# Casts of head pairs 2 to 5 on VectorE, and the first loads of batch 1 and the first-half weights re-ordered, in a hash-attention kernel with a maxout FFN

## The chip, the cores and the metric

The kernel runs on one core of one Trainium2 chip. The metric is the device time of one execution in microseconds (us); lower is better. Engine names: PE is TensorE (PEld its weight loads), DVE is VectorE, ACT is ScalarE, POOL or Pool is GpSimd, SP is SyncE, used here only to issue DMAs. Quoted times are medians of several executions. A ratio is the mean time of one kernel's fast runs over the mean of the other's fast runs in the same rounds, so it is not quite the ratio of the quoted medians. "Fast" leaves out executions more than 1.5% above the fastest of the same kernel. A profile is one execution; its span is 1.7 to 1.8 us shorter than the time measured for it.

## The reference

Inputs are q, k, v of 4 batches x 8 heads x 768 positions x 64, a random projection of 64 x 6, and FFN weights. Positions attend only where the six sign bits of q and k projected agree.

```python
def _attn_ref(q, k, v, proj):
    q_bits = (np.einsum('bhsd,dk->bhsk', q, proj) > 0)
    k_bits = (np.einsum('bhsd,dk->bhsk', k, proj) > 0)
    # ... bucket = sum of bits * powers of two
    mask = q_bucket[:, :, :, None] == k_bucket[:, :, None, :]
    scores = np.where(mask, scale * np.matmul(q, k.transpose(0, 1, 3, 2)), -1e9)
    attn = np.exp(scores - scores.max(-1, keepdims=True))
    attn = attn / (attn.sum(-1, keepdims=True) + 1e-09)
    return np.matmul(attn, v)

def _moe_ref(x, w1, w2, w3, w_out):        # x: 3072 x 512
    h = np.maximum(np.maximum(x @ w1, x @ w2), x @ w3)
    return h @ w_out
```

## The kernel before

The work runs in 16 head pairs, numbered 0 to 15 (four per batch). While pair n goes through its score matmuls and exponentials, the kernel finishes the softmax of pair n-1, hashes pair n+1, and transposes and casts the operands of pair n+2. FFN matmuls of a finished batch fill PE from pair 4 on. A pair has 12 units (one 768-wide exponential each on ACT), and `add(u, f, ...)` places a piece of work behind unit u. The kernel schedules by hand, and in the timelines below the instructions of an engine come in this program order.

Three chains matter here. The first is the operand of a pair: DMA to `nat`, transpose to `tf` (fp32), then a cast to bf16 into the operand tile.

```python
    def load(nm, b, j):                    # batches 1 to 3: four DMAs on the Pool queue
        t = natp.tile([P, 4, R * D // 4], FP32, tag=nm + "nat", name=nm + "nat")
        for hd in (0, 1):
            # ...
                nc.gpsimd.dma_start(t[32 * g : 32 * g + 32, ...], s[...])

    def convert(nm, b, j, cs=slice(0, S), copy=nc.gpsimd.tensor_copy):
        for hd in (0, 1):
            copy(oset(b, j)[nm, hd][head_rows(hd), cs], tf[nm, b, j][head_rows(hd), cs])
```

The second is the hash: matmul into two PSUM banks, threshold on DVE into `bt`, then eight small DMAs (12 x 384 bf16 each) on the SP queue into spare rows of the operand tiles. The second half's writes are needed from the second unit of the pair on.

```python
    def hash_pair(b, j):
        # ... 16 matmuls into ps[0], ps[1]
        for half in (0, 1):
            nc.vector.tensor_scalar(out=bt[:, half_cols(half)], in0=ps[half][:, 0:HS], ...)
            for hd in (0, 1):
                for z, nm in enumerate(("q", "k")):
                    nc.sync.dma_start(oset(b, j)[nm, hd][...], bt[...])
```

The third is the softmax denominator: ones-matmuls on PE, eviction `ds` on ACT, a reciprocal `rc` on DVE, eight tiny copies `r` on Pool, a broadcast `rb` on DVE, and the scaled product `xT` on DVE.

```python
    def den_rc(ph):
        nc.vector.transpose(dT..., rcb.pop(ph)[:])
        # ...
        nc.vector.reciprocal(rc[:], rc[:])
        for half in (0, 1):
            # ... four copies per half
                    nc.gpsimd.tensor_copy(r2[o : o + 32, :], rc[s : s + 32, :])
```

`hold` is a tiny Pool copy which reads what a DMA wrote, and so keeps everything behind it on the Pool queue back until that DMA has landed. `hold` at the end of pair 0 is called "the gate" below: it waits for the last hash write of pair 1 before the first loads of batch 1 are issued.

```python
        if ph == 0:
            # ...
            add(11, hold, (oset(0, 1)["k", 1][0:1, S - 1 : S], slice(0, 1)))
            add(11, load, "k", 1, 0)
            add(11, load, "q", 1, 0)
        elif ph == 1:
            add(5, load_v, 0, 1)
            add(5, load, "k", 1, 1)
            add(5, load, "q", 1, 1)
            for m in range(3):
                add(7, load_weight, m, 0)
        elif ph == 2:
            add(6, load_v, 0, 2)
            add(6, load_v, 0, 3)
        elif ph == 3:
            # ... loads of pair 6, then
            for m in range(3):
                add(7, load_weight, m, 1)
```

The softmax here doesn't subtract the row's maximum and nothing guards it: scores larger than these inputs give would overflow.

Of the kernel before, what the change touches and what calls it, by code (L numbers as in the profile page):

```python
# [17 lines left out]
def kernel(  # L18
# [12 lines left out]
    nc = tc.nc  # L31
    B, H, S, D = q.shape
# [4 lines left out]
    HS = S // 2  # L37
# [4 lines left out]
    NPAIR = H // 2  # L42
# [23 lines left out]
    def half_cols(half):  # L66
        return slice(half * HS, half * HS + HS)

    def head_rows(hd):
        return slice(D * hd, D * hd + D)  # L70
# [99 lines left out]
    def oset(b, j):  # L170
        return opd[(b * NPAIR + j) % NSET]
# [30 lines left out]
    def split_psum(wide):  # L202
        psx.close()
        n = 1 if wide else 2
        extra = psx.enter_context(tc.tile_pool(name=f"psx{n}", bufs=n, space=bass.MemoryType.PSUM))
        sc_ring.clear()
        sc_ring.extend((psp, psp, extra) if wide else (psp, psp))
        bank_ring.clear()
        bank_ring.extend((psw, psw) if wide else (psw, psw, extra, extra))
# [34 lines left out]
        src = nat[nm, b, j][:].rearrange("p pg (c x) -> p c pg x", x=D)[:, :, :, 0:32]  # L244
        nc.vector.transpose(dst.rearrange("p (c pg i) -> p c pg i", pg=4, i=32), src)  # L245

    def convert(nm, b, j, cs=slice(0, S), copy=nc.gpsimd.tensor_copy):
        for hd in (0, 1):
            copy(oset(b, j)[nm, hd][head_rows(hd), cs], tf[nm, b, j][head_rows(hd), cs])  # L249

# [36 lines left out]
    def qk_unit(ph, b, j, half, c):  # L287
        sc = psum2()
        for hd in (0, 1):
            rows = KROWS[hd]  # L290
            kT = oset(b, j)["k", hd]
            qT = oset(b, j)["q", hd]
            nc.tensor.matmul(sc[:, hd, 0:HS], kT[rows, c * P : c * P + P],  # L293
                             qT[rows, half * HS : half * HS + HS], start=True, stop=True)
        nc.scalar.activation(atile(ph, half, c)[:, :, 0:HS], sc[:, :, 0:HS], ActFn.Exp, scale=SCALE)  # L295
# [120 lines left out]
    h0, h1 = half_cols(0), half_cols(1)  # L416
    vcopy, acopy = nc.vector.tensor_copy, nc.scalar.copy
    pe_transpose("k", 0, 0, 0, vcopy)
    pe_transpose("q", 0, 0, 0, acopy)
    hash_first("k", 0)  # L420
    convert("k", 0, 0, h0, acopy)
    hash_first("q", 0)
    convert("q", 0, 0, h0, acopy)
    pe_transpose("k", 0, 0, 1, vcopy)
    pe_transpose("q", 0, 0, 1, acopy)
# [3 lines left out]
    for ph, (b, j) in enumerate(pairs):  # L429
        todo = {u: [] for u in range(NU)}  # L430

        def add(u, f, *a):
            todo[u].append(lambda: f(*a))

        def prep(nb, nj):
            if nb == 0:
                for u, nm, half in ((4, "k", 0), (5, "k", 1), (6, "q", 0), (8, "q", 1)) if ph else ((7, "k", 0), (8, "k", 1), (9, "q", 0), (10, "q", 1)):
                    add(u, pe_transpose, nm, nb, nj, half, nc.vector.tensor_copy)
                    if half == 1:
                        add(u, convert, nm, nb, nj)  # L440
            else:
                for u, nm in zip((1, 5) if ph < NPAIR else (8, 10), ("k", "q")):
                    add(u, transpose, nm, nb, nj)
                    add(u, convert, nm, nb, nj)

        if ph > 0:
            pb, pj = pairs[ph - 1]
            sparse = ph <= NPAIR
            if sparse:
                add(2, den_mm, ph - 1, 0, NT3)  # L450
                add(3, den_mm, ph - 1, NT3, NCH)
                add(4, den_rc, ph - 1)
                add(5, den_rb, ph - 1, 0)
                add(6, den_rb, ph - 1, 1)
                if ph == NPAIR:
                    add(7, split_psum, False)
                add(7, av, ph - 1, pb, pj, 0)
                add(9, av, ph - 1, pb, pj, 1)
            else:
                add(1, den_mm, ph - 1, 0, NCH)  # L460
                add(2, den_rc, ph - 1)
                add(4, den_rb, ph - 1, 0)
                add(5, den_rb, ph - 1, 1)
                add(6, av, ph - 1, pb, pj, 0)
                add(6, av, ph - 1, pb, pj, 1)
        if ph == 0:
            add(0, hold, nat["q", 0, 1][:, 0:1])
            add(0, load_v, 0, 0)
            add(3, load0, "k", 3, nc.gpsimd)
            add(3, load0, "q", 3, nc.gpsimd)  # L470
            add(11, hold, (oset(0, 1)["k", 1][0:1, S - 1 : S], slice(0, 1)))
            add(11, load, "k", 1, 0)
            add(11, load, "q", 1, 0)
        elif ph == 1:
            add(5, load_v, 0, 1)
            add(5, load, "k", 1, 1)
            add(5, load, "q", 1, 1)
            for m in range(3):
                add(7, load_weight, m, 0)
        elif ph == 2:  # L480
            add(6, load_v, 0, 2)
            add(6, load_v, 0, 3)
        elif ph == 3:
            add(6, load, "k", *pairs[6])
            add(6, load, "q", *pairs[6])
            for m in range(3):
                add(7, load_weight, m, 1)
        elif ph + 3 < len(pairs):
            add(6, load, "k", *pairs[ph + 3])
            add(6, load, "q", *pairs[ph + 3])  # L490
            if ph == 4:
                add(8, load_wo)
        if 4 <= ph + 1 < len(pairs):
            add(9, load_v, *pairs[ph + 1])
        if 0 < ph and ph + 1 < len(pairs):
            add(0 if ph <= NPAIR else 1, hash_pair, *pairs[ph + 1])
        if ph + 2 < len(pairs):
            prep(*pairs[ph + 2])
        u = 0
        order = [(c, half) for c in range(NCH) for half in (0, 1)]  # L500
        if ph == 0:
            order = [(c, half) for half in (0, 1) for c in range(NCH)]
            add(0, hash_first, "k", 1)
            add(0, convert, "k", 0, 0, h1)
            for i, (nm, half) in enumerate((("k", 0), ("k", 1), ("q", 0), ("q", 1))):
                add(2 + i // 2, pe_transpose, nm, 0, 1, half, vcopy if half == 0 else acopy)
            add(1, hash_first, "q", 1)
            add(1, convert, "q", 0, 0, h1)
            add(4, hash_pair, 0, 1)
            add(4, convert, "k", 0, 1)  # L510
            add(4, convert, "q", 0, 1)
        if ph == 1:
            split_psum(True)
        for c, half in order:
            qk_unit(ph, b, j, half, c)
            for f in todo[u]:
                f()
            left = len(pairs) * NU - (ph * NU + u)
            quota = (ffn_left[0] - TAILW) / left
            spent = 0.0  # L520
            while ffn and spent + ffn[0][0] / 2 <= quota:
                cost, f = ffn.popleft()
                f()
                spent += cost
            ffn_left[0] -= spent
            u += 1
# [41 lines left out]
```

## Time and profile before

| | before |
|---|---|
| time at the prediction | 301.31 us median (300.43 to 301.68) |
| span of the profile | 298.9 us |
| PE busy | 281.0 us (94%) |
| DVE, ACT, POOL busy | 159.5, 191.7, 152.9 us |
| PE busy from 100 to 220 us | 119.75 of 120 us |

First the page of the kernel before: busy us with share of the span and instructions, then rows of 40 equal slices of the span, one digit each (busy tenths for PE and POOL, granted TensorE clock in tenths for PEclk).

```profile
PE 281.0 (94%) x2220; PEld 146.4 (49%) x2220; DVE 159.5 (53%) x346; ACT 191.7 (64%) x290; POOL 152.9 (51%) x353
...
PE   7987897985999899999999999999999999999994
...
POOL 7698895696776575748373938384252020200000
PEclk9999797996999999999999999999999999999999
```

Behind the tenth slice (75 us) PE is full. Only the front has room, and there Pool is the engine with the high digits.

Next the table of windows of the kernel before: start:end, length, then busy us of PE, PEld, DVE, ACT and POOL with their instruction counts, the granted clock (1.00 is full), the DMA engines' busy share and GB/s.

```profile
24.00:28.00 4.00, 3.67 (x40) 1.80 (x38) 1.27 (x4) 3.96 (x7) 3.64 (x8) 1.00 0.59 153
28.00:32.00 4.00, 1.99 (x16) 1.45 (x17) 2.10 (x5) 1.57 (x3) 3.66 (x13) 0.92 1.02 221
32.00:36.00 4.00, 4.00 (x25) 1.90 (x22) 1.46 (x4) 1.63 (x2) 3.22 (x6) 0.65 1.09 217
48.00:52.00 4.00, 4.00 (x28) 1.00 (x32) 2.29 (x4) 0.88 (x2) 1.94 (x3) 0.57 0.57 80
56.00:60.00 4.00, 4.00 (x43) 1.84 (x40) 3.24 (x7) 3.58 (x6) 3.09 (x9) 1.00 0.03 7
68.00:72.00 4.00, 1.43 (x5) 0.71 (x5) 2.71 (x5) 0.75 (x2) 3.53 (x11) 0.62 1.32 207
72.00:76.00 4.00, 4.00 (x20) 1.58 (x18) 0.79 (x3) 1.36 (x2) 0.94 (x3) 0.53 1.21 235
```

Three times PE idles and the clock then falls to about half. Each half-clock stretch costs again, since a PE that is 4.00 of 4.00 busy at 0.53 does about half the work: a score matmul takes 0.53 us there and 0.33 at full clock.

The PE timeline of the kernel before shows what ended these waits, and a shorter one for a hash write (start us, length, engine, line, operation, output <- inputs; in brackets the idle time before it and its releaser):

```profile
23.62 0.32 PE L293 MATMUL sc<-qop_1_171,kop_1_169 128*128 128x384 bf16 x1 [0.71 <-DMA qop_1_171<-bt]
...
30.89 0.35 PE L346 MATMUL wk<-at_181,v 128*64 128x385 f16 x2 [1.84 <-DVE ktf L239]
47.94 1.66 PE L271 MATMUL wk<-qtf,pmq 64*32 64x384 f32 x6 [1.62 <-DVE sv L349]
70.57 0.48 PE L364 MATMUL wk<-xT,w_sb 128*128 128x384 f16 x1 [3.40 <-DVE xT L352]
```

And the Pool timeline of the kernel before shows why DVE was late, with `r` the reciprocal copies:

```profile
24.48 2.22 POOL L97 DMA_DIRECT2D knat<-in_k_dram  x4
26.69 2.19 POOL L97 DMA_DIRECT2D qnat<-in_q_dram  x4
28.87 0.91 POOL L330 COPY r_522<-rc 32x12 f32<-32x12 f32 x4
...
43.48 0.83 POOL L249 CAST kop_1_169<-ktf 64x768 bf16<-64x768 f32 x1
44.37 0.89 POOL L330 COPY r_718<-rc 32x12 f32<-32x12 f32 x4
...
66.62 0.70 POOL L105 DMA_DIRECT2D v<-in_v_dram  x1 [0.56 <-DMA knat<-in_k_dram]
67.36 0.89 POOL L330 COPY r_1046<-rc 32x12 f32<-32x12 f32 x4
```

The reciprocals were ready at 27.7, 42.1 and 64.8 us. The copies started 1.2, 2.3 and 2.5 us later, behind load issues, casts, and a v load whose issue had to wait for an earlier load to land.

### The profile page before, as it was taken

The numbers are of one execution on the slowest core, as the hardware profiler recorded it, in microseconds if no ns is written. First come the engines' busy times: TensorE is split into PE (matmuls) and PEld (weight loads), VectorE is DVE, ScalarE is ACT, GpSimd is POOL, SyncE is SP. The second block draws the span as 40 slices with busy tenths as digits, with TensorE's granted clock in tenths as the row PEclk, the third lists the DMA queues.
The fourth block names the chain that finished last, engine by engine and source line by source line (L and its number), as shares of the span: only waits on it lengthen the run. The fifth ranks groups of instructions, "written<-read, shape, count | busy, mean of one in ns | idle before, by whom it ended". The sixth has DMA issues, their size and how long they took to land.

```text
span 298.9 us, 6145 instructions
## 1 busy us (share of the span) xinstructions
PE 281.0 (94%) x2220; PEld 146.4 (49%) x2220; DVE 159.5 (53%) x346; ACT 191.7 (64%) x290; POOL 152.9 (51%) x353
## 2 busy tenths in 40 slices
PE   7987897985999899999999999999999999999994
PEld 3543442432455445554555555554555455555551
DVE  4843546534575718573675547672757063725250
ACT  3787395982568695868767776768676966131322
POOL 7698895696776575748373938384252020200000
PEclk9999797996999999999999999999999999999999
DMA  7945997089996293719282848276012020020202
GB/s 174 170 114 144 216 176 111 15 200 220 208 182 138 69 242 94 165 30 203 114 197 33 194 142 196 37 163 168 14 29 37 27 81 2 0 105 2 106 0 106
DMA packets 26718, 34.54 MB, mean 116 GB/s; under 512 B 10080, under 2 KB 20736, under 8 KB 26688
## 3 DMA queue, kind: packets, MB, share of 16 engines
q0 software_dynamic: 14704, 24.39, 40.7%
q1 hardware_dynamic: 9648, 8.85, 9.7%
q10 hardware_dynamic: 2336, 0.92, 1.4%
q8 instruction: 17, 0.28, 0.4%
q14 instruction: 13, 0.11, 0.1%
HBM read 33.03 MB, written 6.29 MB: 132 GB/s over the span
## 4 chain that ended last, share of the span: by engine, by line
PE 81%; POOL 7%; DVE 4%; DMA 4%; issue 1%; ACT 1%; SPq 0%; ACTq 0%; DVEq 0%; POOLq 0%
PE wk L364 32%; PE sc L293 18%; PE wk L380 10%; PE wk L346 10%; PE wk L309 5%; PE wk L271 4%; DMA knat<-in_k_dram 2%; DMA pr<-in_proj_dram 1%; POOL knat L97 1%; PE wk L238 1%; PE wk L256 1%; POOL w_sb L188 1%; POOL qnat L97 1%; DVE qtf L245 1%; DMA kop_1_169<-bt 1%
## 5 line engine op out<-in xcount | busy, mean ns | idle before, releaser
L364 PE MATMUL wk<-xT,w_sb 128*128 128x384 f16 x576 | 111.9, 327 | 3.9 <-DVE xT L352 3.4
L364 PEld LDWEIGHTS <-w_sb 128*128 128x128 f16 x576 | 54.4, 98 | 46.2 <-issue 11.3
L274 DVE TENSOR_SCALAR bt<-wk,thrqk,fac 128x384 bf16<-128x384 f32 x30 | 18.9, 673 | 44.0 <-PE wk L271 44.0
L346 PEld LDWEIGHTS <-v 128*64 128x64 f16 x384 | 21.3, 112 | 16.6 <-issue 9.1
L97 POOL DMA_DIRECT2D qnat<-in_q_dram x48 | 26.3, 553 | 4.9 <-DMA w_sb<-in_moe_w_dram 3.1
L97 POOL DMA_DIRECT2D knat<-in_k_dram x48 | 26.5, 559 | 0.0
L293 PE MATMUL sc<-qop_0_168,kop_0_167 76*128 76x384 bf16 x72 | 24.0, 333 | 1.9 <-ACT at_183 L295 0.6
L293 PE MATMUL sc<-qop_0_165,kop_0_163 128*128 128x384 bf16 x72 | 23.9, 332 | 0.3 <-ACT qtf L239 0.3
L394 ACT COPY o<-wk 128x512 f32<-128x512 f32 x23 | 13.5, 586 | 13.8 <-PE wk L380 13.2
L293 PE MATMUL sc<-qop_1_174,kop_1_173 76*128 76x384 bf16 x60 | 20.5, 341 | 0.9 <-POOL kop_2_179 L249 0.5
L293 PE MATMUL sc<-qop_1_171,kop_1_169 128*128 128x384 bf16 x60 | 20.4, 340 | 0.7 <-DMA qop_1_171<-bt 0.7
L293 PE MATMUL sc<-qop_2_180,kop_2_179 76*128 76x384 bf16 x60 | 19.7, 328 | 0.4 <-ACT at_185 L295 0.4
L293 PE MATMUL sc<-qop_2_177,kop_2_175 128*128 128x384 bf16 x60 | 19.6, 327 | 0.0
L320 DVE STREAM_TRANSPOSE dT<-ds 128x384 f32<-128x384 f32 x16 | 9.2, 572 | 14.7 <-ACT ds L315 14.7
L271 PE MATMUL wk<-qtf,pmq 64*32 64x384 f32 x120 | 14.8, 509 | 1.6 <-DVE sv L349 1.6
L309 PEld LDWEIGHTS <-ones_157 128*32 128x32 f16 x384 | 8.8, 96 | 10.2 <-issue 7.2
L271 PE MATMUL wk<-ktf,pmk 64*32 64x384 f32 x120 | 13.4, 518 | 0.0
L295 ACT ACTIVATE at_188<-sc 128x768 f16<-128x768 f32 x8 | 6.7, 836 | 9.8 <-PE sc L293 9.8
L295 ACT ACTIVATE at_200<-sc 128x768 f16<-128x768 f32 x8 | 6.6, 821 | 9.8 <-PE sc L293 9.8
L293 PEld LDWEIGHTS <-kop_1_173 76*128 76x128 bf16 x60 | 6.0, 99 | 12.7 <-issue 8.2
L349 DVE TENSOR_SCALAR sv<-wk 128x1 f32<-128x1 f32 x32 | 4.9, 153 | 13.2 <-PE wk L346 13.2
L105 POOL DMA_DIRECT2D v<-in_v_dram x16 | 11.6, 727 | 0.6 <-DMA knat<-in_k_dram 0.6
(481 smaller groups left out, 672.1 us busy)
## 6 DMA issues: line engine op xcount, KB each, us to landing
knat<-in_k_dram POOLq DMA_DIRECT2D x48, 176.0 KB, 3.7
qnat<-in_q_dram POOLq DMA_DIRECT2D x48, 176.0 KB, 4.9
out_dram<-o SPq DMA_DIRECT2D x7, 768.0 KB
v<-in_v_dram POOLq DMA_DIRECT2D x16, 192.0 KB, 3.6
w_sb<-in_moe_w_dram POOLq DMA_DIRECT2D x6, 384.0 KB, 7.5
wo_sb<-in_moe_w_out_dram POOLq DMA_DIRECT2D x1, 768.0 KB, 8.6
out_dram<-o SPq DMA_DIRECT2D x2, 256.0 KB
knat_94<-in_k_dram SPq DMA_DIRECT2D x2, 192.0 KB
```

The source lines that it names most:

```text
L97: nc.gpsimd.dma_start(t[32 * g : 32 * g + 32, :, 0 : NCH * D - 32], s[:, :, 32 * blk : 32 * blk + NCH * D - 32])
L105: nc.gpsimd.dma_start(t[:].rearrange("p h c d -> p h (c d)"), v[b, 2 * j : 2 * j + 2].rearrange("h (p c) d -> p h (c d)", p=P))
L271: nc.tensor.matmul(ps[half][o : o + 32, 0:HS], pm[nm][head_rows(hd), :], tf[nm, b, j][head_rows(hd), half_cols(half)], start=True, stop=True)
L274: nc.vector.tensor_scalar(out=bt[:, half_cols(half)], in0=ps[half][:, 0:HS], scalar1=thr["qk"][:, 0:1], scalar2=fac[:, 0:1], op0=AluOp.is_ ...
L293: nc.tensor.matmul(sc[:, hd, 0:HS], kT[rows, c * P : c * P + P], qT[rows, half * HS : half * HS + HS], start=True, stop=True)
L295: nc.scalar.activation(atile(ph, half, c)[:, :, 0:HS], sc[:, :, 0:HS], ActFn.Exp, scale=SCALE)
L309: nc.tensor.matmul(ps[32 * g : 32 * g + 32, 0:HS], ones32[:], atile(ph, half, c)[:, hd, 0:HS], start=(c == 0), stop=(c == NCH - 1))
L320: nc.vector.transpose(dT[:].rearrange("p a x -> p (a x)"), rcb.pop(ph)[:])
L346: nc.tensor.matmul(ps[D * hd : D * hd + D, 0 : HS + 1], vv[:, hd, c, :], atile(ph, half, c)[:, hd, :], start=(c == 0), stop=(c == NCH - 1))
L364: nc.tensor.matmul(ps[:, 0:HS], w_sb[m, fb // NT3][:, jc, (fb % NT3) * P : (fb % NT3) * P + P], xT[b][:, jc, half * HS : half * HS + HS], ...
L380: nc.tensor.matmul(ps[:, 0:DM], hts[b, half, fb][:, t * P : t * P + P], w_sb["o"][:, fb, :], start=(fb == 0), stop=(fb == NFB - 1))
L394: nc.scalar.copy(o[:, t, :], ps[:, 0:DM])
```

## The change

The intent is to empty the Pool queue where the reciprocal copies stand in it. Casts of pairs 2 to 5 go to DVE. The q load of batch 1's first pair goes behind the copies. The gate opens on the first half's hash write, so that the k load need not wait for the second. First-half weights move from pair 1 to pair 2, in front of v of pairs 2 and 3; second-half weights move one unit later in pair 3. (The casts of pair 1 and of half of pair 0 stay on Pool; they are named explicitly because the default changed.)

```diff
--- before.py
+++ after.py
@@ -244,7 +244,9 @@
         src = nat[nm, b, j][:].rearrange("p pg (c x) -> p c pg x", x=D)[:, :, :, 0:32]
         nc.vector.transpose(dst.rearrange("p (c pg i) -> p c pg i", pg=4, i=32), src)
 
-    def convert(nm, b, j, cs=slice(0, S), copy=nc.gpsimd.tensor_copy):
+    def convert(nm, b, j, cs=slice(0, S), copy=None):
+        if copy is None:
+            copy = nc.vector.tensor_copy if b * NPAIR + j < 6 else nc.gpsimd.tensor_copy
         for hd in (0, 1):
             copy(oset(b, j)[nm, hd][head_rows(hd), cs], tf[nm, b, j][head_rows(hd), cs])
 
@@ -468,23 +470,23 @@
             add(0, load_v, 0, 0)
             add(3, load0, "k", 3, nc.gpsimd)
             add(3, load0, "q", 3, nc.gpsimd)
-            add(11, hold, (oset(0, 1)["k", 1][0:1, S - 1 : S], slice(0, 1)))
+            add(11, hold, (oset(0, 1)["k", 1][0:1, HS - 1 : HS], slice(0, 1)))
             add(11, load, "k", 1, 0)
-            add(11, load, "q", 1, 0)
         elif ph == 1:
+            add(5, load, "q", 1, 0)
             add(5, load_v, 0, 1)
             add(5, load, "k", 1, 1)
             add(5, load, "q", 1, 1)
+        elif ph == 2:
             for m in range(3):
-                add(7, load_weight, m, 0)
-        elif ph == 2:
+                add(6, load_weight, m, 0)
             add(6, load_v, 0, 2)
             add(6, load_v, 0, 3)
         elif ph == 3:
             add(6, load, "k", *pairs[6])
             add(6, load, "q", *pairs[6])
             for m in range(3):
-                add(7, load_weight, m, 1)
+                add(8, load_weight, m, 1)
         elif ph + 3 < len(pairs):
             add(6, load, "k", *pairs[ph + 3])
             add(6, load, "q", *pairs[ph + 3])
@@ -501,14 +503,14 @@
         if ph == 0:
             order = [(c, half) for half in (0, 1) for c in range(NCH)]
             add(0, hash_first, "k", 1)
-            add(0, convert, "k", 0, 0, h1)
+            add(0, convert, "k", 0, 0, h1, nc.gpsimd.tensor_copy)
             for i, (nm, half) in enumerate((("k", 0), ("k", 1), ("q", 0), ("q", 1))):
                 add(2 + i // 2, pe_transpose, nm, 0, 1, half, vcopy if half == 0 else acopy)
             add(1, hash_first, "q", 1)
-            add(1, convert, "q", 0, 0, h1)
+            add(1, convert, "q", 0, 0, h1, nc.gpsimd.tensor_copy)
             add(4, hash_pair, 0, 1)
-            add(4, convert, "k", 0, 1)
-            add(4, convert, "q", 0, 1)
+            add(4, convert, "k", 0, 1, slice(0, S), nc.gpsimd.tensor_copy)
+            add(4, convert, "q", 0, 1, slice(0, S), nc.gpsimd.tensor_copy)
         if ph == 1:
             split_psum(True)
         for c, half in order:
```

## The prediction

> **What bounds it now.** The page gives PE 281.0 of 298.9 us busy (94%); the chain of waits is 81% PE. From 100 us to 220 us the table of windows shows PE busy 119.75 of 120. So the back is PE-bound; a gain can only come from the front, pairs 1 to 4 (21 to 80 us), where PE idles and loses its clock. The same table shows the granted clock at 0.50 to 0.85 in 30-36, 48-52 and 68-76 us, each time after an idle stretch.
>
> Why PE idles: the Pool queue is in order and nearly full in pairs 1 to 4 (13.2 of 15.3, 8.7 of 9.4, 7.6 of 13.1, 16.3 of 21.5 us). The small reciprocal copies (8 x 0.19 us) wait behind casts (0.83 us) and DMA issues (0.55 to 0.77 us):
> - Pair 1: reciprocal ready 27.7, copies start 28.87 behind eight load issues; PE idles 28.9-30.9, then runs at half clock.
> - Pair 2: ready 42.1, copies 44.37, behind casts and weight issues; the next hash starts 47.94 (1.6 us idle, then half clock).
> - Pair 4: ready 64.8, copies 67.36. Pool was held at 66.3 until a k load eight issues earlier had landed. PE waits 3.4 us for xT (ACT 4.7), and the clock is 0.50 until 75 us.
>
> **What changes.** 16 casts of 64x768 (pairs 2 to 5; 16 x 0.88 = 14 us) leave Pool; DVE gets 16 copies. No such DVE copy is in the trace. The Trainium skill ("VectorE: DVE Perf Modes", Mode 2x_2P) says a single-source SBUF-to-SBUF copy runs two elements a cycle even for fp32: estimate 0.5 us each, 8 us in all; at one a cycle, 0.9. DVE is 42 to 65% busy in these pairs, but the casts sit between the reciprocal work and the evictions. "SBUF — State Buffer" (two separate sides) says such a copy and a Pool instruction exclude each other; no trace here shows it yet; I allow 1 us. Moreover: q of batch 1's first pair is issued after the copies; the gate waits for the first half's hash write (about 3 us sooner); first-half weights go behind pair 2's copies. Total DMA work is unchanged.
>
> **By stage (estimates from these times).**
> - Pair 1: copies 1.1 us earlier, no clock drop, hash at about 35 instead of 36.85.
> - Pair 2: copies when the reciprocal is ready (40.2); end of the next hash 46.5 instead of 50.2.
> - Pair 3: the added DVE casts stand before the second rb and xT: gives back about 1 us.
> - Pair 4: copies at about 62 instead of 67.4; first FFN block 65 instead of 70.6 (5.5 us), plus up to 2.6 us of half clock.
> Behind that everything is shifted, not changed. Gain 5 to 8.5 us, less contention: 6.7 us.
>
> **Predicted:** 294.6 us, 8 in 10 between 290.8 and 299.5. Faster by over 2%: 0.55; within: 0.42; slower: 0.03.
>
> **What would show it.** DVE casts of about 0.5 us; Pool's wait in pairs 1 to 4 for the reciprocal rather than the reverse; PE's 3.4 us wait for xT under 2; clock 1.00 in 30-36 and 48-52 us; PE still near 120 of 120 in the middle.
>
> **What would make it wrong.** DVE casts of 0.9 us or more, from no fast mode or from Pool holding the port, making DVE the new wait for rb and xT. Earlier k loads colliding with the second-half hash writes (needed at pair 1's second unit). Loads for pair 2's v queued behind 1.2 MB of weights (about 6 us) and landing after need (near 51 us). PE's gap before the FFN still long enough to halve the clock.

## The result, and the profile after

| | before | after |
|---|---|---|
| time, rounds of the prediction | 301.22 us (300.43 to 301.68) | 297.17 us (296.63 to 297.81) |
| ratio of fast runs, 95% interval | | 0.987 (0.984 to 0.990) |
| span of the profile | 298.9 us | 295.9 us |
| PE busy | 281.0 us | 279.6 us |
| DVE busy | 159.5 us | 169.5 us |
| POOL busy | 152.9 us | 140.6 us |

The kernel was 1.3% faster in these rounds. Two later sets, on two different chips, gave 0.997 (0.993 to 1.002) and 0.993 (0.988 to 0.997) for the same two kernels, so the gain is somewhere between nothing and 1.3%. All are "within 2%".

The page of the changed kernel, the same rows as above:

```profile
PE 279.6 (95%) x2220; PEld 145.7 (49%) x2220; DVE 169.5 (57%) x362; ACT 191.8 (65%) x290; POOL 140.6 (48%) x337
...
PE   8978798798999999999999999999999999999994
...
POOL 7591855567684847566573937383242020200000
PEclk9997999799999999999999999999999999999999
```

The clock dips at other places now, at the fourth and eighth slice. The table of windows of the changed kernel:

```profile
24.00:28.00 4.00, 3.05 (x21) 0.81 (x24) 0.84 (x2) 1.58 (x3) 0.00 (x0) 0.62 0.42 98
32.00:36.00 4.00, 2.97 (x27) 1.70 (x28) 3.85 (x9) 1.82 (x3) 3.96 (x8) 1.00 0.56 142
48.00:52.00 4.00, 3.68 (x42) 1.24 (x46) 2.91 (x6) 2.38 (x5) 0.72 (x2) 1.00 1.31 204
56.00:60.00 4.00, 4.00 (x26) 1.75 (x24) 3.24 (x7) 1.23 (x2) 3.96 (x9) 0.61 0.58 157
72.00:76.00 4.00, 4.00 (x31) 2.28 (x28) 2.61 (x5) 2.56 (x5) 2.96 (x5) 1.00 1.06 236
```

All three old stretches (32, 48, 72 us) run at 1.00. But 24-28 us and 56-60 us, full speed before, are now at 0.62 and 0.61. The PE timeline of the changed kernel shows two waits that did not exist, or were half as long:

```profile
24.95 0.48 PE L295 MATMUL sc<-qop_1_171,kop_1_169 128*128 128x384 bf16 x1 [1.38 <-DMA qop_1_171<-bt]
...
48.31 1.32 PE L273 MATMUL wk<-qtf,pmq 64*32 64x384 f32 x6 [1.01 <-DVE sv L351]
...
55.78 0.53 PE L348 MATMUL wk<-at_181,v 128*64 128x385 f16 x2 [1.38 <-DMA v<-in_v_dram]
...
69.99 0.32 PE L366 MATMUL wk<-xT,w_sb 128*128 128x384 f16 x1 [0.86 <-DVE xT L354]
```

The chain of waits of the changed kernel names the transfers behind them (start us, length, what):

```profile
21.51 3.40 DMA qop_1_171<-bt
...
47.27 8.46 DMA v<-in_v_dram
```

The first is the hash write of pair 1's second half. Before, the same write was issued at 21.70 and PE stopped waiting for it at 23.62, so it took at most 1.9 us. In 23 to 25 us, while PE waited for this write or had just got it, the windows of the changed kernel show the DMA engines 1.00 and 0.98 busy, where the kernel before shows 0.07 and 0.04. The second is v of pair 2, queued behind the three weight loads. The Pool timeline of the changed kernel:

```profile
21.05 0.32 POOL L180 CAST gate<-kop_1_169 1x1 f32<-1x1 bf16 x1
21.32 2.35 POOL L97 DMA_DIRECT2D knat<-in_k_dram  x4
30.43 0.88 POOL L332 COPY r_517<-rc 32x12 f32<-32x12 f32 x4 [6.76 <-DVE rc L325]
...
43.31 0.86 POOL L332 COPY r_712<-rc 32x12 f32<-32x12 f32 x4 [1.59 <-DVE rc L325]
45.05 2.27 POOL L188 DMA_DIRECT2D w_sb<-in_moe_w_dram  x3
47.27 1.45 POOL L105 DMA_DIRECT2D v<-in_v_dram  x2
...
66.82 0.87 POOL L332 COPY r_1046<-rc 32x12 f32<-32x12 f32 x4 [2.99 <-DVE rc L325]
```

Pool now waits for the reciprocal everywhere, so the change did what it meant to do. But the reciprocals themselves come late: pair 1's copies begin at 30.43 instead of 28.87, and pair 4's at 66.82, only 0.5 us before the old 67.36. The k load now issues at 21.32, exactly while the hash writes of 21.51 are under way.

Where the 3.0 us of span came from can be read off one point, the first score matmul of pair 5: 78.29 us before, 75.28 after. Behind it both profiles take 220.6 us (298.9 - 78.29 and 295.9 - 75.28). The first FFN block that waits for `xT` in pair 4 moved only 0.6 us (70.57 to 69.99); the other 2.4 us are the clock that no longer halves at 70-76 us.

### The profile page after: what moved, and what is told of

Same layout as the page of the kernel before. It is cut to its first block, busy times and chain, and to the rows that moved or that the text cites. A ratio compares the mean times of both kernels' runs of the same rounds, so it can differ in the third digit from the quotient of the medians.

```text
span 295.9 us, 6133 instructions
## 1 busy us (share of the span) xinstructions
PE 279.6 (95%) x2220; PEld 145.7 (49%) x2220; DVE 169.5 (57%) x362; ACT 191.8 (65%) x290; POOL 140.6 (48%) x337
## 4 chain that ended last, share of the span: by engine, by line
PE 80%; DMA 5%; DVE 5%; POOL 4%; ACT 2%; issue 1%; SPq 1%; DVEq 0%; POOLq 0%; ACTq 0%
PE wk L366 32%; PE sc L295 17%; PE wk L382 11%; PE wk L348 10%; PE wk L311 5%; DMA v<-in_v_dram 4%; PE wk L273 3%; PE sc L417 1%; DMA qop_1_171<-bt 1%; POOL qnat L97 1%; SPq L282 1%; POOL w_sb L188 1%; DVE dT L322 1%; PE wk L258 1%; POOL qnat_337 L89 1%
## 5 line engine op out<-in xcount | busy, mean ns | idle before, releaser
L97 POOL DMA_DIRECT2D qnat<-in_q_dram x48 | 26.9, 566 | 2.4 <-DMA v<-in_v_dram 1.5
L295 PE MATMUL sc<-qop_1_171,kop_1_169 128*128 128x384 bf16 x60 | 20.2, 336 | 1.4 <-DMA qop_1_171<-bt 1.4
L273 PE MATMUL wk<-ktf,pmk 64*32 64x384 f32 x120 | 12.8, 495 | 0.0
L295 PEld LDWEIGHTS <-kop_0_167 76*128 76x128 bf16 x72 | 7.1, 98 | 9.5 <-issue 5.7
L245 DVE STREAM_TRANSPOSE ktf<-knat 128x768 f32<-128x768 f32 x12 | 11.6, 970 | 0.0
```

The source lines that it names most:

```text
L97: nc.gpsimd.dma_start(t[32 * g : 32 * g + 32, :, 0 : NCH * D - 32], s[:, :, 32 * blk : 32 * blk + NCH * D - 32])
L273: nc.tensor.matmul(ps[half][o : o + 32, 0:HS], pm[nm][head_rows(hd), :], tf[nm, b, j][head_rows(hd), half_cols(half)], start=True, stop=True)
L295: nc.tensor.matmul(sc[:, hd, 0:HS], kT[rows, c * P : c * P + P], qT[rows, half * HS : half * HS + HS], start=True, stop=True)
```

## The experiments

Theory A: the change removes Pool's delay, but its load half adds two DMA waits, and each costs its idle time and then a stretch at half clock. Rival B: the DVE casts hold the front back, because they stand in front of the hash and of `rb`, and because they exclude Pool from a shared port. Twelve runs, eight of them new kernels, were made in three sets; each set has its own executions of before. Every result was correct.

| run | this, us | before of its set, us | ratio (95%) | granted clock of its executions |
|---|---|---|---|---|
| r0, changed again | 298.59 | 298.25 | 0.997 (0.993-1.002) | 0.986 to 0.993 (one slow at 0.943) |
| e1, late gate | 293.63 | 298.25 | 0.983 (0.979-0.988) | 0.992 to 1.000 |
| e2, v first | 296.44 | 298.25 | 0.992 (0.987-0.996) | 0.992 to 1.000 |
| e3, both | 293.85 | 298.25 | 0.984 (0.980-0.988) | 0.998 to 1.000 |
| e4, casts only | 296.60 | 299.56 | 0.990 (0.985-0.995) | 0.988 to 1.000 |
| e5, loads only | 300.48 | 299.56 | 1.005 (0.999-1.011) | 0.977 to 0.987 |
| e6, casts late | 290.36 | 299.56 | 0.970 (0.965-0.974) | 1.000 |
| r3, changed again | 297.76 | 299.69 | 0.993 (0.988-0.997) | 0.986 to 0.993 |
| e7, e6 with early gate | 292.96 | 299.69 | 0.976 (0.971-0.981) | 0.991 to 1.000 |
| e8, e6 with two casts earlier | 289.78 | 299.69 | 0.967 (0.962-0.972) | 0.997 to 1.000 |

The two other runs, r1 and r2, were single executions of before, for their profiles.

One caution about the third set (r3, e7, e8): the quickest execution of before, 296.26 us, lay outside its rounds, and the ratios count three executions (301.15 to 302.08 us) that the record lists as slow. Over those listed as fast alone, r3 is 0.996, e7 0.980 and e8 0.970.

### The changed kernel again (r0)

No edit; the anchor of the first set.

> The changed kernel again, as the anchor of this set on one chip. Both theories: about 297.2 us, 0.987 of before; PE waits 1.4 us for the hash write of pair 1 and 1.4 us for v in pair 3, the granted clock is half at 25-28 and at 56-59 us.

Measured 298.59 us, ratio 0.997. Its profile fell into a slow execution (303.26 us at a mean clock of 0.943), so its durations are not compared here; its waits are where they were expected, 2.1 us for the hash write and 1.2 us for v. One expectation failed: no half clock followed the wait for v (0.95 at 56-60 us, as in all the stretches around it). That the changed kernel hardly beat before in this set is a result too: on this chip before ran at 298.25 us, not at 301.

### The late gate (e1)

```diff
-            add(11, hold, (oset(0, 1)["k", 1][0:1, HS - 1 : HS], slice(0, 1)))
+            add(11, hold, (oset(0, 1)["k", 1][0:1, S - 1 : S], slice(0, 1)))
```

> The changed kernel, but the first load of batch 1 waits again for the second half's hash write, as before the change. Theory A (two new DMA waits ate the gain): the write of qop_1_171 lands in about 1.9 us instead of 3.4, PE's wait there falls from 1.4 to 0.7 us or less, the clock is 1.00 at 24-28 us, and 2 to 3 us are gained: 294.2 to 295.2 us. Rival B (the casts on DVE are what holds pair 1 back, by the port shared with Pool and by standing before the hash): the wait and the half clock stay, the time stays within 0.7 us of the changed kernel.

Measured 293.63 us beside 298.59: the intervals of the ratios do not meet (0.979 to 0.988 against 0.993 to 1.002). PE's wait for the hash write fell to 0.3 us and the clock at 24-28 us was 1.00. The gain was larger than expected, about 1.4% (4.0 us between the means) instead of 2 to 3 us. Theory A holds for the gate. B fails there: the casts on DVE were untouched. The PE timeline of this version:

```profile
23.94 0.65 PE L295 MATMUL sc<-qop,kop 128*128 128x384 bf16 x3 [0.27 <-DMA qop<-bt]
...
35.31 0.83 PE L273 MATMUL wk<-qtf,pmq 64*32 64x384 f32 x4
```

The second line is the hash after pair 1: it starts at 35.31 us, where the prediction had put it (about 35), and not at 37.64 as in the changed kernel. The copies of pair 1 start at 28.09, also close to the prediction (27.8). PE still waited 1.31 us for v in pair 3, and the clock was 0.50 in 54-56 us. That profile is of the longest of the six executions (295.30 us at 0.992); the others, at 0.998 to 1.000, can't have had much of this.

### v in front of the weights (e2)

```diff
         elif ph == 2:
-            for m in range(3):
-                add(6, load_weight, m, 0)
             add(6, load_v, 0, 2)
             add(6, load_v, 0, 3)
+            for m in range(3):
+                add(6, load_weight, m, 0)
```

> The changed kernel, but v of pairs 2 and 3 is issued in front of the three weight loads of pair 2, not behind them. Theory A: v of pair 2 lands about 6 us earlier (near 50 us), PE's 1.4 us wait for v in pair 3 is gone and the clock stays 1.00 at 56-59 us: 2.5 to 3 us gained, 294.2 to 294.8 us. Rival B: DVE's chain of casts, rb and xT in pair 3 is the next limit at nearly the same time, so the gain is under 1 us and the clock still drops.

Measured 296.44 us, ratio 0.992 against 0.997 for the changed kernel, with intervals that overlap. The wait for v was gone and the clock was 1.00 at 56-60 us, as A said, but the gain was smaller than A said: the means of the two versions differ by 1.7 us, with a 95% interval of about 0.5 to 2.9 worked out from their eleven fast executions. One likely reason: the profiles of the changed kernel in this set (r0) and the last (r3) have no half clock behind the wait for v, so there was little clock to regain. PE now waited 0.9 us for `xT` at each of two hashes; the first of these waits (1.01 us) was there in the changed kernel. The wait for the hash write of pair 1 stayed, 2.58 us in this profile.

### Both (e3)

Both edits above together.

> Both edits. Theory A: the two waits are independent, so the gains add: 291 to 292.5 us, clock 1.00 in all stretches from 24 to 80 us, first FFN block of pair 4 about 5 us earlier than in the changed kernel (near 63.5 us). Rival B: within 1.5 us of the changed kernel.

Measured 293.85 us: no gain over the late gate alone. The clock was 1.00 throughout and neither DMA wait was there, but the first waiting FFN block came at 66.49 us, not near 63.5. The PE timeline of this version shows what took over, one wait in pair 2 and one in pair 3:

```profile
46.16 1.32 PE L273 MATMUL wk<-qtf,pmq 64*32 64x384 f32 x6 [0.95 <-DVE sv L351]
...
57.25 1.33 PE L273 MATMUL wk<-qtf,pmq 64*32 64x384 f32 x6 [0.94 <-DVE xT L354]
```

So A was right about the gate and wrong that the gains add. Behind the wait for v stood DVE: in pairs 2 and 3 the hash waits for `xT`, and the chain from reciprocal to `xT` holds a transpose and two casts. This is the part of B that is true. The chain of waits shows the same write as above landing quickly with the late gate, issued at 22.25:

```profile
22.25 1.87 DMA qop<-bt
```

### Only the casts (e4)

From the kernel before, only the cast part of the diff (the default of `convert`, and the explicit Pool copies for pairs 0 and 1). Loads, gate and weights as before.

> Only the casts moved to DVE; all loads, the gate and the weights stay as before the change. Theory A: neither of the two new DMA waits arises; the reciprocal copies of pair 2 no longer stand behind casts, those of pair 1 still behind eight load issues, those of pair 4 still behind a load that has to land. 1 to 3 us faster than before, so at least as fast as the changed kernel. Rival B (casts on DVE hold the front back): slower than before or equal.

Measured 296.60 us, ratio 0.990. This half alone is as good as the whole change (0.987, 0.997 and 0.993 in its three sets). Its profile has a clock of 1.00 in every window from 20 to 80 us. As A said, pair 2's copies no longer wait behind casts (Pool waits 2.16 us for the reciprocal there), pair 1's still stand behind eight issues (PE waits 1.82 us), and no wait for v appears. One expectation failed: pair 4's copies were not held by a load that had to land, since Pool reached that load sooner; it waited 1.62 us for the reciprocal.

### Only the loads (e5)

```diff
-            copy = nc.vector.tensor_copy if b * NPAIR + j < 6 else nc.gpsimd.tensor_copy
+            copy = nc.gpsimd.tensor_copy
```

(from the changed kernel)

> Only the loads, the gate and the weights moved; the casts stay on Pool. Theory A: with Pool still busy the early gate moves the first load by under 1 us and the copies still wait behind casts: within 1 us of before, and no part of the gain is the loads'. Rival B: this half carries the gain, 3 us or more faster than before.

Measured 300.48 us, ratio 1.005 with 1 just inside the interval: no gain, perhaps a loss. The PE timeline says why:

```profile
29.70 1.17 PE L348 MATMUL wk<-at,v 128*64 128x385 f16 x12 [0.71 <-DVE ktf L239]
...
47.33 1.66 PE L273 MATMUL wk<-qtf,pmq 64*32 64x384 f32 x6 [3.76 <-DVE sv L351]
...
58.30 1.18 PE L348 MATMUL wk<-at,v 128*64 128x385 f16 x12 [2.92 <-DMA v<-in_v_dram]
```

The wait in pair 1 did shrink (0.71 us, from 1.84), because the copies no longer stood behind the q issues. But in pair 2 six casts in a row (38.47 to 43.7 us on Pool) stood in front of copies whose reciprocal had been ready at 39.6, and v came 2.92 us late. The early gate did nothing here, as Pool's casts of pair 2 kept the k load back until 24.57 us anyway; PE's wait for the hash write stayed at 0.85 us. So the two halves of the change are tied: the gate opens early only once the casts are off Pool.

### The casts late, the transpose in DVE's gap (e6)

From e3. Casts of pairs 3 to 5 go behind the first half's `xT`; the transpose of q goes between the reciprocal and the first `rb`; the second `rb` goes behind the first `xT`.

```diff
                     if half == 1:
-                        add(u, convert, nm, nb, nj)
+                        add(10 if ph else u, convert, nm, nb, nj)
             else:
-                for u, nm in zip((1, 5) if ph < NPAIR else (8, 10), ("k", "q")):
+                for u, uc, nm in zip((1, 4) if ph < NPAIR else (8, 10), (8, 10), ("k", "q")):
                     add(u, transpose, nm, nb, nj)
-                    add(u, convert, nm, nb, nj)
+                    add(uc, convert, nm, nb, nj)
@@
-                add(5, den_rb, ph - 1, 0)
-                add(6, den_rb, ph - 1, 1)
+                add(6, den_rb, ph - 1, 0)
                 # ...
                 add(7, av, ph - 1, pb, pj, 0)
+                add(8, den_rb, ph - 1, 1)
```

> From the version with both edits: in pairs 1 to 3 the DVE casts come after the first half's xT, the transpose of q goes between the reciprocal and the first rb, where DVE waited 1.0 us for Pool's copies, and the second rb comes after the first half's xT. Theory: the remaining PE waits of 0.9 us each (hash of pairs 2 and 3 on xT, first FFN block of pair 4 on xT) vanish, 2 to 3 us faster than the version with both edits: about 291 us where that runs 293.8. Rival: the front is bound by ACT (8.9 us of work per pair) and nothing changes: within 0.7 us of it.

Measured 290.36 us (289.73 to 290.75), ratio 0.970: 3% under before, beyond both kernels. The waits of the hashes in pairs 2 and 3 and of the FFN block for `xT` are gone. ACT was not the limit. The edit moves three things at once (twelve of the sixteen casts, the transpose of q, the second `rb`); which of them gave how much was not tested. One longer wait remains in the front, of the denominator matmuls for the eviction of a hash, which now stands behind four casts:

```profile
36.74 0.67 PE L311 MATMUL wk<-at,ones 128*32 128x384 f16 x12 [1.11 <-DVE bt L276]
```

### The early gate again, in the fast version (e7)

The gate line of e1 reversed, in e6.

> The fast version (casts late, v first), but with the early gate of the changed kernel put back. Theory A (the early k load slows the second half's hash writes): the write lands in 3.4 us or more, PE waits 1.4 us or more for it, and 2 to 5 us are lost: 292.5 to 295.5 us where the fast version runs 290.4. Rival (the gate cost only through the DVE casts in front of the hash): within 0.7 us of the fast version.

Measured 292.96 us where e6 ran 290.36 in the set before it, beside befores of nearly the same median (299.69 and 299.56); in its own set it stands against 289.78 of e8, which also differs by the two casts moved in e8. The ratios of e6 and e7 touch (0.965 to 0.974 and 0.971 to 0.981), but the executions of e7 (291.49 to 293.62 us) all lie above those of e6 (289.73 to 290.75), and within its set the means of e7 and e8 differ by 2.9 us (about 1.8 to 4.0). The chain of waits of this version has the hash write again:

```profile
22.04 3.87 DMA qop<-bt
```

and its PE timeline the wait for it:

```profile
25.96 0.98 PE L295 MATMUL sc<-qop,kop 128*128 128x384 bf16 x3 [2.13 <-DMA qop<-bt]
```

The write took 3.87 us again, PE waited 2.13 us and the clock at 24-28 us was 0.77. In the profiles with an early k load this write took 3.4 to 4.2 us; with the late gate it took 1.9. So the early gate has its price in both schedules, with the casts early or late. By which resource the two transfers meet was not tested; what the traces show is DMA engines 0.9 to 1.0 busy while the slow write is under way (23-26 us here).

### Two casts earlier (e8)

In e6, the casts of k in pair 1 at unit 8 instead of 10.

```diff
-                        add(10 if ph else u, convert, nm, nb, nj)
+                        add((8 if nm == "k" else 10) if ph else u, convert, nm, nb, nj)
```

> The fast version, but in pair 1 the casts of k come two units earlier, so that two casts and not four stand before the eviction of the next hash, for which PE waits 1.1 us. Theory: that wait falls by about 1 us and the time by 0.5 to 1.1 us (289.3 to 289.9 where the fast version runs 290.4). Rival: ACT's work per pair takes the gain back: within 0.3 us.

Measured 289.78 us, ratio 0.967 (0.962 to 0.972) against 0.970 (0.965 to 0.974) for e6 in another set. The wait of 1.11 us is gone from its profile, in which PE has no wait over 0.6 us between 20 and 80 us. The difference in time has the expected size but isn't resolved by these intervals. This is the fastest version measured.

### Before once more (r1, r2), and the changed kernel once more (r3)

No edits.

> The kernel before once more, for a second profile of it: is the spread of its times (297.6 to 301.7 us over the sets so far) one of half-clock stretches? If so, a faster execution shows fewer of the three stretches at half clock (30-36, 48-52, 68-76 us) while PE's waits themselves stay where they were; if not, the waits differ.

> One more profile of the kernel before, because its times spread over 4.5 us (297.2 to 301.7) and the two profiles so far are both of slow ones (300.6 and 300.9). If this execution is near 297 to 298 us and the spread is one of half-clock stretches, at most one of the stretches near 30, 48 and 70 us is at half clock, with PE's waits about as before.

> The changed kernel again, beside before: the two sets so far gave ratios of 0.987 and 0.997 whose intervals do not meet. If the clock stretches make the difference, this gives something between, and the profile shows the waits for the hash write (1.4 us or more) and for v (1.2 us or more) again.

Both profiles of before fell on slow executions again (300.93 and 300.80 us), so no profile of a quick one exists, and the direct test failed. They do show that slow executions differ: half clock at 48-54 and near 72-75 us, none near 30, but a longer wait at the hash (2.83 and 2.86 us instead of 1.62). So the waits differ as well, and the spread isn't only one of half-clock stretches. What every execution does record is its mean granted clock, and for before it goes with the time: 296.26 us at 1.000, 297.2 to 299.7 mostly at 0.986 to 0.993, 300.3 to 301.2 at 0.983, 302.08 at 0.976. Most versions at 1.000 spread less (e6: 1.0 us over six executions; before in the same set: 4.5 us), but e8's four executions at 1.000 range from 289.03 to 291.59 us, so the clock isn't all of the spread. What decides in which execution the clock falls was not found.

r3 gave 0.993, between the other two sets, and the two waits again (2.54 us and 1.17 us). The clock was 0.67 and 0.50 in the two windows from 24 to 32 us, behind the first, but 1.00 at 56-60 us, behind the second. So of theory A's two stretches at half clock, the one behind v came in one of three profiles of the changed kernel.

## Why the prediction was right or wrong

The time (297.2 us) lies in the predicted range, and the verdict was one of the two that were thought likely. That is partly luck: the range is 8.7 us wide and reaches to within 2 us of the time before, one of the larger terms failed, and most of the gain came from a single other term. The centre was too low: a gain of 6.7 us was predicted, 4.05 us came in those rounds, and less in the later ones. Point by point, from the two profiles, in us:

| step | before | predicted | after |
|---|---|---|---|
| a DVE cast | - | 0.5 | 0.55 |
| copies in pair 1 | 28.87 | 27.8 | 30.43 |
| hash after pair 1 starts | 36.85 | 35 | 37.64 |
| copies in pair 2 | 44.37 | 40.2 | 43.31 |
| end of the hash after pair 2 | 50.3 | 46.5 | 50.0 |
| from there to the end of the next hash (pair 3) | 10.2 | about 11 | 12.3 |
| copies in pair 4 | 67.36 | 62 | 66.82 |
| first waiting FFN block | 70.57 | 65 | 69.99 |
| half clock regained in pair 4 | - | up to 2.6 | 2.4 |
| from pair 5 to the end | 220.6 | unchanged | 220.6 |

**Right: what bounds it.** PE in the back, Pool's order in the front. Pool now waits for the reciprocal, and the back is the same to 0.1 us.

**Right: the cost of a DVE cast.** The Trainium skill ("VectorE: DVE Perf Modes", Mode 2x_2P and the perf-mode tier table) says that a single-source SBUF copy moves two elements a cycle even for fp32. 768 elements at two a cycle of the 0.96 GHz that the page gives are 0.40 us, at one 0.80 (an estimate from the page). The trace has 0.55 us, so it agrees with two plus a fixed part. Two of the lines of the casts in the changed kernel (count, then min/median/max ns, first and last start):

```profile
L251 DVE CAST kop_2_175<-ktf x2: 557/823/1089, 20.2 to 52.8; 64x768 bf16<-64x768 f32 x2
L251 DVE CAST qop_2_180<-qtf x2: 553/553/553, 22.4 to 56.9; 64x768 bf16<-64x768 f32 x2
```

**Right, and small: the shared port.** "SBUF — State Buffer" (SBUF: two separate sides) says that such a copy and a Pool instruction exclude each other for the whole instruction. The trace agrees where the two met: two of the sixteen casts, at 19.3 and 20.2 us, took 0.92 and 1.09 us while Pool was casting, each ending 0.41 us after the Pool cast beside it, and one Pool cast beside them took 1.04 instead of 0.83. One other took 0.71, the rest 0.55 to 0.58. In sum that is about 1 us, as allowed for. In this profile PE waited 0.59 us for a copy behind the two long casts, a wait that the kernel before did not have. But it did not carry the loss: e1 left the casts where they were (the two took 1.59 us together in its profile) and gained 1.4%, and e2, where they were not stretched (1.12 us), has the longer wait for the hash write.

**Wrong: "Pair 1: copies 1.1 us earlier, no clock drop, hash at about 35".** This is the step that failed, and the sum inherited it. The hash came 0.8 us later than before, not 1.9 us earlier. The early gate lets 0.7 MB of k load run while the last hash writes are in flight. The next write that PE needs took 3.4 us instead of at most 1.9, PE idled 1.38 us, and the clock was 0.62 in 24-28 us. With the late gate (e1) the write took 1.9 us, the clock stayed at 1.00 and the hash started at 35.31, so the rest of the step was right. The prediction named this collision among the things that could make it wrong, but gave it no us. e1 prices it at about 1.4% (0.983 against 0.997), e7 at about 2.6 us (292.96 against e6's 290.36, from two sets).

**Right in kind, too small: pair 3.** The stage gave back about 2 us, not 1. The wait for v that the prediction had also named took 1.38 us and dropped the clock. It landed at 55.7 us; the prediction had put the need near 51, and in the trace PE began to wait at 54.4. e2 and e3 show that this wait is not the whole term: without it DVE's chain with the casts in it is next in line, 0.9 us at each hash.

**Pairs 2 and 4** failed mostly through what came before them. The copies ran as soon as the reciprocal was ready, as predicted, but the reciprocal was late by what pairs 1 and 3 had lost. In pair 4 that is all: from the end of the hash to the copies 4.5 us were predicted and 4.5 came. Pair 2 also fell short by itself: from the hash after pair 1 to the end of the next, 11.5 us were predicted, 12.4 came (13.4 before), and PE waited 1.01 us there for DVE. With the late gate (e1) it is 12.4 again, so this part isn't the gate's. Pair 4's clock term was right (2.4 us), and it is most of the gain seen.

So where did the expected gain go? Into two new waits for DMAs of the load half, the one for the hash write above all, and into DVE's own chain behind them. The cast half alone gives what the whole change gives, as far as the intervals tell (e4), and with the gate late, v first and the casts out of the chain the same idea gives 3% (e6, e8).

## What to carry to other kernels

Before a load is allowed to start earlier, look at which small transfer is in flight at that moment and who needs it next: here an early bulk load about doubled the landing time of a 9 KB write that was needed next, and took back most of what the change gave without it (1.7% in e1, 0.3% in the same set with the early load). When work moves from a full in-order queue to one with room, place it behind the link of the chain that others wait for, not where it stood in the old queue: with the loads in order, the kernel gained 1.6% with the casts in their old places (e3) and 3% with twelve of the sixteen moved behind the first `xT`, together with a transpose and a second `rb` (e6). In this kernel PE waits from 1.31 us up were followed by a stretch at half clock in some executions, and waits of up to 1.90 us were not in others, so count the stretch as a possible second cost, and judge small changes by several sets, since this clock varies from execution to execution.

## What the Trainium skill lacked or had wrong

- "TensorE: Matmul & The Clock Gate" (Part 1) gives an idle window of about 3.4 us as what drops the clock to half. Here it dropped after single waits of 1.31, 1.38, 1.62 and 1.84 us, with PE busy for 1.0 to 1.8 us of the 3.4 us before the end of each. Waits of 1.82 to 1.90 us (e4, r1, r2), with PE busy for 1.0 to 1.1 us of the 3.4, did not drop it. The page's remark that the window runs free would fit such a mix, but no run shows the window.
- "DMA: Bandwidth & Descriptors" has no figure that we found for a small SBUF-to-SBUF write on the SP queue beside a bulk load on the Pool queue. Here a write of 12 x 384 bf16 took 1.9 us with next to no other traffic (DMA engines 0.04 to 0.07 busy in the kernel before) and 3.4 to 4.2 us beside a 0.7 MB load.
- "SBUF — State Buffer" gives one example of a Pool-issued DMA starved by DVE copies, 620 ns grown to about 3100. It has none for the time of the issues themselves. In this trace four load issues on Pool beside two DVE casts of 0.55 us took 2.56 us instead of 2.20.
